# Attention ordered by a list scheduler instead of a table of offsets: a fused attention, mixture and MLP kernel on one core

## The chip, the cores and the metric

The kernel runs on one core of one Trainium2 chip. The metric is the device time of one execution in microseconds (us), from the first to the last instruction on the core with the little that lies around it. Lower is better.

## The reference

The program computes three stages in a row, all in float32:

```
attention: q, k, v of (4 batches, 8 heads, 576 positions, 64), gates f
  scores = q k^T / 8 + cum_i - cum_j        cum = cumsum(log(clip(f)))
  causal mask, softmax over the keys, attn v
x = 2304 tokens x 512                       (heads side by side)
mixture:  P = exp(x w_gate - max); 8 times: rows / sum, columns / sum, * N / E
  out = sum over 8 experts of P[:, e] * (relu(x w1[e]) w2[e])      512 -> 1024 -> 512
MLP:      leaky_relu(out w_in) w_out                               512 -> 2048 -> 512
```

## The kernel before, in words

**Matmul in halves.** TensorE multiplies in a rounded format (`fp32r`), so each float32 operand is kept as a high part and a low part, and a product is three matmuls. Every operand therefore costs a rounding copy (ACT, or a CAST on DVE) and a subtraction (DVE or POOL).

**Attention** runs over 32 heads `n`, one after the other and overlapped. The steps of a head are small functions:

- `qk_load` (DMA), then `k_split` with `k1` and `q1` (CASTs on DVE), `k2` and `q1l` (subtractions on POOL, L392 and L401). A DMA (L396) copies `q1` into another tile.
- `qk` (six score tiles `x`, PE, L444 and L445, into the ring `ps_s` of 4 PSUM tiles), `qk_min` (mask and row minimum, DVE, L456), `qk_exp` (ACT, L469).
- `tr` (four groups `u` of transposes, PE, L495, into the ring `ps_t` of 2 PSUM tiles), `tr_hi` (copy out, ACT, L502), `tr_lo` (low part, DVE, L511, only for heads from 10 on; it is the last reader of the `ps_t` tile).
- `pv` (two groups, PE, L531, in `ps_s`), `pv_copy` (ACT), `pv_add` (DVE, L559, heads from 10 on).

For each pair of heads follow `v_load`, `v_split` (a CAST on DVE, L426, and a subtraction on POOL, L428, pairs from 10 on), `recip` (DVE, L573 to L575), `spread` (POOL, L580), `norm_t` (PE, L589) and `norm_m` (DVE, L595), `x_hi` (ACT), `x_lo` (POOL, L614), `x_store` (DMA), `gate` (PE, L640, L641, in `ps_t`) and `gate_add` (DVE, L649 to L651). Heads below 10 (`EARLY`) multiply in plain float32 in `pv`, and so need no `tr_lo`, `pv_add` and `v_split`.

**Filling products.** The first products of the mixture are cut into 168 pieces of four matmuls, `fill_l1` (L206, 384 columns) and `fill_l2` (L233, 512 columns). Pieces are put between attention's steps so that PE has work while it waits; the ones that are left are scheduled behind attention. Three pieces make a group, whose sum is read by ACT (`high`, or `end`) and DVE (`low` L215, or `end` L239). Their weights are split by ACT (L163) and POOL (L167).

**What sets the order.** The program is written in one order, and each engine works through its own instructions in that order; it waits at each for what it needs. For attention this order comes from tables: each step has an offset in units of a head (`HEAD_E` and `PAIR_E` below head 10, `HEAD_T` and `PAIR_T` from there on), `at(n, t, fn)` puts the step at `n + t`, and all are sorted by that number. Four pieces per head are put at the offsets `FILL_T`, from head 10 on, with their readers (`fill_end`) 0.222 later.

Behind attention (`lg_t`, then the Sinkhorn iterations, then the 56 units of mixture and MLP at L1169) the order is made by a list scheduler, `run_events`: each event has its engine, a duration, its needs and a due time, and the earliest that can start is taken, unless a more urgent one can start soon. That part is not changed.

Of the kernel before, what the change touches and what calls it, by code (L numbers as in the profile page):

```python
# [20 lines left out]
P = 128  # L21
B, H, S, D = 4, 8, 576, 64
# [41 lines left out]

FILL_T = (0.208, 0.376, 0.635, 0.861)
FILL_LAG = 0.222
FILL_FROM = 10


EARLY = 10  # L70
HEAD_E = dict(
    load=-1.126, k1=-0.643, k2=-0.073, q1=-0.639, q1l=-0.339, qk0=-0.040, qk1=0.047,
# [13 lines left out]
FILL_E = (0.05, 0.2, 0.35, 0.5, 0.65, 0.8, 0.95)  # L86


def f(ap):
    return ap.bitcast(F32)  # L90
# [7 lines left out]
def moe_kernel(ctx, tc, qT, kT, v, fg, w_gate, w1, w2, w_in, w_out, out):  # L98
    nc = tc.nc
# [6 lines left out]
    wpa = pool("wpa", 8)  # L106
# [48 lines left out]
    def w_hi(src, pool_):  # L155
        t = pool_.tile([P, 2, FG], F32R, tag="w", name="w")
        hi, lo = t[:, 0, :], t[:, 1, :]
        if len(src.shape) == 3:
            s2 = src.shape[2]
            hv, lv = (t.rearrange("p (k c) -> p k c", c=s2) for t in (hi, lo))  # L160
        else:
            hv, lv = hi, lo
        nc.scalar.activation(hv, src, AF.Copy)  # L163
        return hv, lv

    def w_lo(src, hv, lv):
        nc.gpsimd.tensor_tensor(lv, src, f(hv), ALU.subtract)  # L167
# [50 lines left out]
    fh, fpair, fwait = {}, [], set()  # L218
# [57 lines left out]

    fills = list(fill_steps())

    FIRST = 6 + 2 * (FC + TPB) * 3

    def fill(limit=10 ** 9):
        if fills and n_fills - len(fills) < limit:
            for fn in fills.pop(0)[1]:
                fn()

    n_fills = len(fills)

    def fill_end():
        while pend:
            for fn in pend.pop(0):  # L290
                fn()
        fwait.clear()


    with ExitStack() as actx:
# [79 lines left out]

        ops = {}

        def k_split(n, op):
            rq, rk = raws[n]
# [3 lines left out]
            q1, k1, q2, k2 = ops[n]  # L383
            if op == "k1":
                if n:
                    c_ = ca[n:n + 1] if n == 1 else cd[n]
                    nc.sync.dma_start(out=f(q2[D + 2:D + 4, :]), in_=f(c_))
                    nc.sync.dma_start(out=f(k2[D:D + 2, :]), in_=f(c_))
                nc.vector.tensor_copy(k1, rk)
            elif op == "k2":  # L390
                e = nc.gpsimd if n else nc.vector
                e.tensor_tensor(k2[0:D], rk[0:D], f(k1[0:D]), ALU.subtract)  # L392
            elif op == "q1":
                if n:
                    nc.vector.tensor_copy(q1, rq)
                    nc.sync.dma_start(out=f(q2[0:D]), in_=f(q1[0:D]))  # L396
                else:
                    nc.scalar.activation(q1, rq, AF.Copy)
                    nc.scalar.activation(q2[0:D], rq[0:D], AF.Copy)
            else:  # L400
                (nc.gpsimd if n else nc.vector).tensor_tensor(  # L401
                    q1[D:], rq[D:], f(q1[D:]), ALU.subtract)
# [248 lines left out]
                nc.vector.tensor_tensor(dst, ps[0:2 * E], dst, ALU.add)  # L651


        NH = B * H
        todo = []

        def at(n, t, fn, *args):
            todo.append((n + t, len(todo), fn, args))

        for n in range(NH):  # L660
            T = HEAD_E if n < EARLY else HEAD_T
            if n > 1:
                at(n, T["load"], qk_load, n)
            if n:
                for op in ("k1", "k2", "q1", "q1l"):
                    at(n, T[op], k_split, n, op)
            for x in range(6):
                at(n, T[f"qk{x}"], qk, n, x)
                at(n, T[f"mn{x}"], qk_min, n, x)
                at(n, T[f"ex{x}"], qk_exp, n, x)  # L670
            for u in range(4):
                at(n, T[f"t{u}"], tr, n, u)
                at(n, T[f"hi{u}"], tr_hi, n, u)
                at(n, T[f"lo{u}"], tr_lo, n, u)
            for r in range(2):
                at(n, T[f"pv{r}"], pv, n, r)
                at(n, T[f"cp{r}"], pv_copy, n, r)
                at(n, T[f"ad{r}"], pv_add, n, r)
            if n % 2 == 0:
                T = PAIR_E if n < EARLY else PAIR_T  # L680

                V = PAIR_E if n < EARLY + 4 else T
                if n:
                    at(n, V["vload"], v_load, n)
                for op, fn in (("st", stat), ("rc", recip), ("rb", spread), ("xs", x_hi),
                               ("xl", x_lo), ("xd", x_store)):
                    at(n, T[op], fn, n)
                for op in ("vp", "vl"):
                    at(n, V[op], v_split, n, op)
                for r in range(2):  # L690
                    at(n, T[f"nt{r}"], norm_t, n, r)
                    at(n, T[f"nm{r}"], norm_m, n, r)
                    at(n, T[f"ga{r}"], gate, n, r)
                    at(n, T[f"gb{r}"], gate_add, n, r)
# [4 lines left out]
        at(2, 0.05, gate_prep)  # L699
# [13 lines left out]

        for x, fn in enumerate((lg_t, fill, fill)):
            at(NH, 3.2 + 0.01 * x, fn)
        for _, _, fn, args in sorted(todo, key=lambda x: x[:2]):
            fn(*args)
        fill_end()

# [552 lines left out]
    acc_last, tiles = {}, []  # L1272
    nom = {}

    def fill_main(x, fn):
        fn()
        fwait.clear()
        if pend:
            held[x] = pend.pop()

    def fill_part(x, n):
        held[x][n]()

    held = {}
    S_ = "start"
    for x, (dur, fns) in enumerate(fills):
        for fn in fns:
# [392 lines left out]
```

## Time and profile before

| | |
|---|---|
| three runs | 2028.80, 2029.66, 2029.81 us; median 2029.66 us |
| the profiled execution | 2029.37 us |
| its span (first to last instruction) | 2027.6 us |
| around the span | 1.77 us |
| TensorE's granted clock, mean | 1.000 of full speed |
| matmuls in the trace | 11600 |

"Busy" counts an engine's instructions without gaps. A matmul's end is modelled and overlaps the next one's start, so a gap in PE's work shows shorter than it is; the time from one start to the next is the safer measure. In brackets a row names the idle time ahead of it and what ended it.

### The profile page before, as it was taken

To read this page: it belongs to the slowest core of one execution; us is meant where nothing else is said; L and a number is where in the kernel's file an instruction comes from. 1 tells how busy PE (TensorE), PEld (TensorE's weight loads), DVE (VectorE), ACT (ScalarE), POOL (GpSimd) and SP (SyncE) were. 2 spreads that over 40 slices of the span, in tenths; PEclk is the share of its full clock that TensorE was granted. 3 is DMA by queue.
4 is the path that set the end of the run, shared out by engine and by line. 5 is a ranking of instruction groups with operands and counts; after the bars stand their busy time and mean duration, and the time that the engine had idled before them with its cause. 6 is when DMAs were issued, how large, how long until landed. Compare 5 with 4: busy or idle time off the path is not lost.

```text
span 2027.6 us, 32145 instructions
## 1 busy us (share of the span) xinstructions
PE 1990.3 (98%) x11600; PEld 1941.6 (96%) x11600; DVE 1759.2 (87%) x2423; ACT 983.6 (49%) x1752; POOL 1169.5 (58%) x734
## 2 busy tenths in 40 slices
PE   7999999999999999999999999999999999999999
PEld 6788888999999999999999999999999999999999
DVE  6799985789798999999998989889898989888766
ACT  6887774554444443433343334434333356655443
POOL 4676655646666567666565655656575474455302
PEclk9999999999999999999999999999999999999999
DMA  4654545777887777777767777777677755766563
GB/s 134 176 155 130 152 122 183 271 266 259 271 300 276 242 259 258 244 241 250 245 242 239 274 248 246 248 242 255 239 264 247 249 208 194 263 229 235 182 208 139
DMA packets 145622, 460.54 MB, mean 227 GB/s; under 512 B 15912, under 2 KB 42168, under 8 KB 145464
## 3 DMA queue, kind: packets, MB, share of 16 engines
q1 hardware_dynamic: 145460, 458.48, 66.9%
q8 instruction: 93, 1.52, 0.3%
q14 instruction: 65, 0.53, 0.1%
q10 hardware_dynamic: 4, 0.00, 0.0%
HBM read 402.76 MB, written 51.08 MB: 224 GB/s over the span
## 4 chain that ended last, share of the span: by engine, by line
PE 87%; DVE 9%; issue 2%; ACT 1%; DMA 0%; POOL 0%; SPq 0%; DVEq 0%; ACTq 0%; POOLq 0%
PE x L1169 42%; PE y L1169 32%; PE ps_pv L531 3%; PE ps_m L233 2%; PE ps_t L495 2%; PE ps_m L206 1%; PE ps_s L444 1%; PE ps_s L445 1%; DVE ps_s L456 1%; DVE hl L1240 1%; PE y L233 1%; DVE ptl L511 1%; PE x L206 1%; DVE acc_C L1252 1%; PE y L206 1%
## 5 line engine op out<-in xcount | busy, mean ns | idle before, releaser
L1169 PE MATMUL x<-xw,w 128*128 128x384 f32 x2676 | 500.8, 334 | 2.0 <-DVE xw L923 1.4
L1169 PE MATMUL x<-hh,w 128*128 128x384 f32 x1792 | 490.9, 334 | 2.1 <-DVE w L991 1.7
L1169 PEld LDWEIGHTS x<-xw,w 128*128 128x128 f32 x2676 | 467.0, 188 | 3.7 <-DVE xw L923 2.0
L1169 PE MATMUL y<-xw,w 128*128 128x384 f32 x2004 | 375.0, 334 | 2.6 <-DVE u L1211 1.8
L1169 PE MATMUL y<-hh,w 128*128 128x384 f32 x1344 | 368.0, 334 | 0.0
L1169 PEld LDWEIGHTS y<-xw,w 128*128 128x128 f32 x2004 | 349.5, 188 | 3.6 <-DVE u L1211 2.4
L991 POOL TENSOR_TENSOR w<-wr,w 128x512 fp32r<-128x512 f32 x158 | 251.3, 1595 | 162.6 <-ACT w L163 149.8
L1169 PEld LDWEIGHTS x<-hh,w 128*128 128x128 f32 x1792 | 326.6, 188 | 3.1 <-DVE w L991 2.4
L1169 PE MATMUL x<-hl,w 128*128 128x384 f32 x896 | 299.6, 334 | 1.1 <-DVE hl L1240 0.9
L1169 PEld LDWEIGHTS y<-hh,w 128*128 128x128 f32 x1344 | 245.0, 188 | 0.3 <-issue 0.3
L1169 PE MATMUL y<-hl,w 128*128 128x384 f32 x672 | 224.7, 334 | 0.1
L1252 DVE TENSOR_TENSOR acc_C<-x,acc_C 128x768 f32<-128x768 f32 x177 | 168.4, 952 | 36.6 <-PE x L1169 33.8
L163 ACT ACTIVATE w<-wr 128x512 fp32r<-128x512 f32 x288 | 175.8, 621 | 25.1 <-PE y L1169 17.4
L1252 DVE TENSOR_TENSOR acc_C<-y,acc_C 128x768 f32<-128x768 f32 x148 | 141.0, 953 | 51.9 <-PE y L1169 50.6
L1169 PEld LDWEIGHTS x<-hl,w 128*128 128x128 f32 x896 | 168.2, 188 | 2.0 <-DVE hl L1240 1.5
L1236 ACT ACTIVATE hh<-spare 128x768 fp32r<-128x768 f32 x84 | 71.1, 846 | 147.8 <-PE x L1169 56.9
L1236 ACT ACTIVATE hh<-u 128x768 fp32r<-128x768 f32 x91 | 77.0, 846 | 131.4 <-PE y L1169 82.0
L1240 POOL TENSOR_TENSOR hl<-k,hh 128x768 fp32r<-128x768 f32 x40 | 79.5, 1989 | 97.7 <-ACT hh L1236 97.6
L1236 ACT ACTIVATE hh<-k 128x768 fp32r<-128x768 f32 x112 | 94.7, 846 | 82.3 <-PE x L1169 48.6
L1169 PEld LDWEIGHTS y<-hl,w 128*128 128x128 f32 x672 | 126.1, 188 | 0.7 <-DVE hl L1240 0.7
L1236 ACT ACTIVATE hh<-c 128x768 fp32r<-128x768 f32 x70 | 59.3, 847 | 131.8 <-PE y L1169 82.0
L1205 ACT ACTIVATE u<-x 128x768 f32<-128x768 f32 x91 | 74.1, 814 | 96.1 <-PE x L1169 82.9
(253 smaller groups left out, 3830.4 us busy)
## 6 DMA issues: line engine op xcount, KB each, us to landing
xw<-xo_t SPq DMA_DIRECT2D x208, 768.0 KB
xw<-xo_b SPq DMA_DIRECT2D x154, 768.0 KB
wr<-in_w_dram SPq DMA_DIRECT2D x88, 512.0 KB
pb<-prow SPq DMA_DIRECT2D x44, 384.0 KB
xo_t<-xw SPq DMA_DIRECT2D x16, 768.0 KB
rq<-in_qT_dram SPq DMA_DIRECT2D x64, 144.0 KB
rk<-in_kT_dram SPq DMA_DIRECT2D x64, 144.0 KB
xo_b<-xw SPq DMA_DIRECT2D x12, 768.0 KB
```

The lines of the kernel that those rows point to most:

```text
L163: nc.scalar.activation(hv, src, AF.Copy)
L206: nc.tensor.matmul(ps, w_[:, fs], x_[k][:, xs], start=(x == 0), stop=(x == 11))
L233: nc.tensor.matmul(ps, h_[:, ts], w_, start=(x == 0), stop=(x == 11))
L444: nc.tensor.matmul(o, q1[:, q0:q0 + m], k1[:, k0:k9], start=True, stop=False)
L495: nc.tensor.transpose(ps[:KV[j], c:c + m], prb[n, i][:m, j * P:j * P + KV[j]], ident[:m, :m])
L531: nc.tensor.matmul(ps[:, a - ra:rb - ra], vp, s[:KV[j], o:o + rb - a], start=(x == 0), stop=(x == len(todo) - 1))
L991: ENG[e].tensor_tensor(lo, blk(g, which, WSRC[which][n]), f(hi), ALU.subtract)
L1169: nc.tensor.matmul(o_, w[:, k, w_], m[:, k, :], start=a and k + y == 0, stop=z and k == 1 and y == 2, skip_group_check=True)
L1205: nc.scalar.activation(ctile(u, name, name, bufs), pview(u, p), AF.Copy)
L1236: nc.scalar.activation(hi, tmp[u, LSRC[l]], AF.Copy)
L1240: ENG[e].tensor_tensor(lo, tmp[u, LSRC[l]], f(hi), ALU.subtract)
L1252: nc.vector.tensor_tensor(a, pview(u, l), a, ALU.add)
```

## The change

The tables' offsets no longer set the order. Each step of attention becomes an event `hv(name, how, fn, need, ring, rel, due)`: its engine and duration (`M` PE, `A` ACT, `V` DVE, `P` POOL, `D` DMA; `VP` is DVE using the SBUF port that it shares with POOL), all steps that must be over before it, for PE steps the PSUM ring that it takes a tile of and who releases the tile, and a due time, which is still worked out from the old tables. The pieces and their readers become events of the same kind, with a due time behind all others. `run_heads` then plays the five engines forward: at each turn it takes, over all engines, the event that can start first, where one that is due earlier and can start within a little (`LOOKM` 0.12 us on PE, one instruction elsewhere) goes ahead. Events are then written out in that order.

Two DMAs that were part of `k_split` (`rows`, `q_rows`) become steps of their own. Nothing that is computed changes, and no instruction is added to or taken from PE.

Counted in the order of the two programs on PE: ahead of `lg_t` stand 103 pieces before and 87 now; between the first `qk` of head 11 and the first `qk` of head 31 it is 78 before (48 of `fill_l1`, 30 of `fill_l2`) and 71 now (44 and 27). The other pieces stand behind attention.

Cut to its core:

```diff
-FILL_T = (0.208, 0.376, 0.635, 0.861)
-FILL_LAG = 0.222
-FILL_FROM = 10
+LOOKM, LOOKE = 0.12, 1.0
...
-        def at(n, t, fn, *args):
-            todo.append((n + t, len(todo), fn, args))
...
-                for op in ("k1", "k2", "q1", "q1l"):
-                    at(n, T[op], k_split, n, op)
...
-        for n in range(FILL_FROM, NH + 3):
-            for t in FILL_T if n < NH else FILL_E:
-                at(n, t, fill, FIRST if n < 2 * H + 3 else 10 ** 9)
-                at(n, t + FILL_LAG, fill_end)
...
-        for _, _, fn, args in sorted(todo, key=lambda x: x[:2]):
-            fn(*args)
...
+        BUFS = dict(s=4, t=2, m=2, xt=2)
+        def hv(name, how, fn, *args, need=(), ring=None, rel=(), due=None, t=0.0):
+            hvs[name] = (how, fn, args, [m for m in need if m in hvs], ring, rel, due, t)
...
+                hv(("k1", n), ("VP", 0.39, 0.08), k_split, n, "k1", need=[("load", n)] + old)
+                hv(("k2", n), ("P", 1.41, 0.05), k_split, n, "k2", need=[("k1", n)])
+                hv(("q1", n), ("VP", 0.39, 0.08), k_split, n, "q1", need=[("load", n)] + old)
...
+                hv(("tr", n, u), ("M", M_TR[u], 0.17), tr, n, u,
+                   need=[("ex", n, x) for x in range(6) if XI[x] in TUSE[u]]
+                   + [("pv", n - 2, r) for r in range(2)],
+                   ring="t", rel=[(lo, n, u)], due=place(n, T[f"t{u}"]))
...
+                hv(("lo", n, u), ("V", V_LO[u], 0.07), tr_lo, n, u, need=[("hi", n, u)])
...
+            hv(("rc", n), ("V", 0.5, 0.1), recip, n,
+               need=[("ex", n + y, x) for y in range(2) for x in range(6)])
...
+                    hv(F, ("M", 0.88 if l2_ else 0.71, 0.2), fill_main, x, fn, need=list(dict.fromkeys(need)),
+                       ring="m" if q == 0 else None, rel=[fowner], due=1e6 + x)
...
+        def run_heads():
...
+                        s_ = max(r, free[e])
+                        if how[0] in ("VP", "P"):
+                            s_ = max(s_, port["P" if e == "V" else "V"])
+                        here.append((s_, due[x], x))
...
+                    here.sort(key=lambda k: k[:2])
+                    k = here[0]
+                    for y in here[1:]:
+                        long = hvs[k[2]][0][1]
+                        look = LOOKM if e == "M" else LOOKE * long
+                        if y[1] < k[1] and y[0] < k[0] + look and (e == "M" or y[1] + slip < k[0] + long):
+                            k = y
...
+            for _, x in order:
+                hvs[x][1](*hvs[x][2])
+            return stop
...
+        del fills[:run_heads() + 1]
+        lg_t()
```

Three places show what this does to DVE's queue; lines of the changed kernel have other numbers for the same functions (L453 is `qk_min`, L387 and L393 the CASTs of `k1` and `q1`, L508 `tr_lo`, L646 `gate_add`).

The first place is the start. DVE before, from the end of the part ahead of the loop over heads to the CASTs of head 1 (`k_264`, `q_263`):

```order
L392 TENSOR_TENSOR k_0_227<-rk,k_238 64x576
L456 ISA ps_s,st<-ps_s,mask 96x288
L456 ISA st 96x1
L456 ISA ps_s<-ps_s,mask 96x288
L456 ISA ps_s 96x1
L460 TENSOR_TENSOR st<-st,ps_s 96x1
L389 CAST k_264<-rk 128x576
L395 CAST q_263<-rq 128x576
```

And DVE of the change at the same place, where head 1's tiles are `q_254` and `k_255`:

```order
L390 TENSOR_TENSOR k_0_227<-rk,k_238 64x576
L393 CAST q_254<-rq 128x576
L387 CAST k_255<-rk 128x576
L453 ISA ps_s,st<-ps_s,mask 96x288
L453 ISA st 96x1
```

Head 1's two CASTs moved ahead of head 0's first two `qk_min`.

The second place is head 4, one of the early heads; heads 6 and 8 read alike. DVE before, from the CASTs for head 5 to the first `gate_add` (L649):

```order
L389 CAST k_625<-rk 128x576
L395 CAST q_624<-rq 128x576
L456 ISA ps_s,st<-ps_s,mask 128x128
L456 ISA st 128x1
L456 ISA ps_s,st<-ps_s,mask 128x256
L456 ISA st 128x1
L573 TENSOR_TENSOR st<-st 96x2
L574 TENSOR_SCALAR st<-st 128x10
L575 RECIPROCAL st<-st 128x10
L649 COPY lgT<-ps_g 16x288
```

DVE of the change in head 4, from the same `qk_min` on (`q_706` and `k_707` belong to head 6):

```order
L453 ISA ps_s,st<-ps_s,mask 128x128
L453 ISA st 128x1
L453 ISA ps_s,st<-ps_s,mask 128x256
L453 ISA st 128x1
L646 COPY lgT<-ps_g 16x288
L453 ISA ps_s,st<-ps_s,mask 128x384
L453 ISA st 128x1
L646 COPY lgT<-ps_g 16x288
L453 ISA ps_s,st<-ps_s,mask 96x512
L453 ISA st 96x1
L393 CAST q_706<-rq 128x576
L387 CAST k_707<-rk 128x576
```

CASTs and `recip` no longer stand ahead of `gate_add`; `recip` went to the end of head 3, and the CASTs now serve the head after next. On PE, heads 4 to 9 read the same in both programs.

The third place is head 21, one of the late heads. DVE before, from the end of the first two `qk_min` on (the CAST is for head 22):

```order
L460 TENSOR_TENSOR st<-st,ps_s 96x1
L559 TENSOR_TENSOR xs<-ps_pv,xt 64x320
L456 ISA ps_s,st<-ps_s,mask 128x128
L456 ISA st 128x1
L395 CAST q_2820<-rq 128x576
L511 TENSOR_TENSOR ptl<-ps_t,pth 128x480
L511 TENSOR_TENSOR ptl<-ps_t,pth 128x448
L239 TENSOR_TENSOR acc<-ps_m,acc 128x512
L426 CAST vp<-rv_194 128x5x2x64
L456 ISA ps_s,st<-ps_s,mask 128x256
L456 ISA st 128x1
L511 TENSOR_TENSOR ptl<-ps_t,pth 128x512
```

DVE of the change from the end of head 21's first two `qk_min` on:

```order
L457 TENSOR_TENSOR st<-st,ps_s 96x1
L508 TENSOR_TENSOR ptl<-ps_t,pth 128x480
L508 TENSOR_TENSOR ptl<-ps_t,pth 128x448
L453 ISA ps_s,st<-ps_s,mask 128x256
L453 ISA st 128x1
L453 ISA ps_s,st<-ps_s,mask 128x128
L453 ISA st 128x1
L453 ISA ps_s,st<-ps_s,mask 128x384
L453 ISA st 128x1
L508 TENSOR_TENSOR ptl<-ps_t,pth 128x512
L592 TENSOR_TENSOR xs<-xs,ps_r 128x256
L423 CAST vp<-rv_194 128x5x2x64
```

The CAST of `q1` left its place ahead of `tr_lo`; it stands at the end of head 21 now, right ahead of the next head's first `qk_min`. In heads 18, 20 and 22 the three instructions of `recip` stand between the first two `qk_min`, a few instructions ahead of `tr_lo`.

## Rows read from the trace of the kernel before

**Rows 1.** The page, part 1: busy time of each engine, share of the span, instructions.

```profile
PE 1990.3 (98%) x11600; PEld 1941.6 (96%) x11600; DVE 1759.2 (87%) x2423; ACT 983.6 (49%) x1752; POOL 1169.5 (58%) x734
```

**Rows 2.** Windows: length, then busy PE, PEld, DVE, ACT, POOL (instructions), clock, DMA.

```profile
0.00:8.33 8.33, 0.00 (x0) 0.00 (x0) 5.05 (x10) 4.60 (x6) 4.48 (x16) 1.00 0.58 162
...
23.94:84.17 60.23, 57.91 (x361) 47.44 (x361) 41.56 (x149) 48.10 (x158) 31.43 (x29) 1.00 0.51 144
...
91.86:287.00 195.14, 185.22 (x1223) 165.34 (x1222) 181.55 (x538) 153.39 (x446) 138.22 (x116) 1.00 0.55 148
287.00:318.85 31.85, 31.52 (x188) 28.32 (x188) 17.25 (x45) 17.65 (x41) 13.74 (x11) 1.00 0.33 105
...
345.00:2027.60 1682.60, 1669.54 (x9590) 1660.47 (x9589) 1480.41 (x1582) 732.00 (x1028) 957.43 (x545) 1.00 0.70 243
```

**Rows 3.** Waits of PE from 91.86 to 287: total us, times, longest.

```profile
PE ps_t L495 <- DVE ptl L511: 8.7, 13, 1.3
```

**Rows 4.** Timeline around 190 (POOL, DVE, PE): start, duration, instruction, idle before.

```profile
190.73 1.42 POOL L392 TENSOR_TENSOR k<-rk,k 64x576 fp32r<-64x576 f32 x1
...
190.79 1.68 DVE L395 CAST q<-rq 128x576 fp32r<-128x576 f32 x1
...
192.39 1.18 DVE L511 TENSOR_TENSOR ptl<-ps_t,pth 128x480 fp32r<-128x480 f32 x2
...
193.18 0.63 PE L495 MATMUL ps_t<-ident,p 128*128 128x128 f32 x5 [0.80 <-DVE ptl L511]
```

**Rows 5.** DVE in groups by shape, 91.86 to 287: busy us, mean ns.

```profile
L395 DVE CAST q<-rq 128x576 fp32r<-128x576 f32 x20 | 15.5, 774 | 0.0
...
L389 DVE CAST k<-rk 128x576 fp32r<-128x576 f32 x20 | 12.4, 618 | 0.0
...
L215 DVE SCALAR_TENSOR_TENSOR hl<-ps_m,hh 128x384 fp32r<-128x384 f32 x16 | 8.8, 548 | 0.6 <-ACT hh L214 0.6
...
L573 DVE TENSOR_TENSOR st<-st 96x2 f32<-96x2 f32 x10 | 5.3, 528 | 0.0
```

**Rows 6.** Timeline of DVE, instances of the same instructions elsewhere.

```profile
55.35 0.46 DVE L389 CAST k<-rk 128x576 fp32r<-128x576 f32 x1
55.73 0.45 DVE L395 CAST q<-rq 128x576 fp32r<-128x576 f32 x1
...
56.69 1.14 DVE L573 TENSOR_TENSOR st<-st 96x2 f32<-96x2 f32 x1
...
203.09 0.23 DVE L573 TENSOR_TENSOR st<-st 96x2 f32<-96x2 f32 x1
```

**Rows 7.** Timeline of PE: first qk of heads 6 to 8, and a wait.

```profile
53.70 0.38 PE L444 MATMUL ps_s<-k,q 128*96 128x288 f32 x1
...
58.65 0.38 PE L495 MATMUL ps_t<-ident,p 96*128 96x96 f32 x2 [0.67 <-DVE lgT L651]
...
61.75 0.38 PE L444 MATMUL ps_s<-k,q 128*96 128x288 f32 x1
...
68.94 0.38 PE L444 MATMUL ps_s<-k,q 128*96 128x288 f32 x1
```

**Rows 8.** Timeline of PE: a wait in head 1, first qk of heads 22 and 23.

```profile
15.58 0.56 PE L445 MATMUL ps_s<-k,q 68*96 68x288 f32 x1 [0.68 <-POOL k L392]
...
198.92 0.37 PE L444 MATMUL ps_s<-k,q 128*96 128x288 f32 x1
...
207.65 0.37 PE L444 MATMUL ps_s<-k,q 128*96 128x288 f32 x1
```

**Rows 9.** Timeline of PE behind attention: pieces in a row.

```profile
326.20 2.24 PE L206 MATMUL x<-xp,w 128*128 128x384 f32 x12
328.28 0.85 PE L206 MATMUL y<-xp,w 128*128 128x384 f32 x4
...
339.30 0.39 PE L233 MATMUL y<-w,hl 128*128 128x512 f32 x1
339.53 0.62 PE L233 MATMUL y<-w,hh 128*128 128x512 f32 x2
```

More of the change, by code (lines that the diff above doesn't have):

```diff
@@ L85 @@
 XOPS = ("b11", "b21", "t2", "t3", "t1", "b22", "t4")
-FILL_E = (0.05, 0.2, 0.35, 0.5, 0.65, 0.8, 0.95)
 def f(ap):
@@ L277, in moe_kernel, with fill_main, fill_part @@
     fills = list(fill_steps())
[L279 to L286, printed above, removed]
+    held = {}
+    def fill_main(x, fn):
+        fn()
+        fwait.clear()
+        if pend:
+            held[x] = pend.pop()
+    def fill_part(x, n):
+        held[x][n]()
     def fill_end():
@@ L376, in moe_kernel, with head_ops @@
         ops = {}
-        def k_split(n, op):
-            rq, rk = raws[n]
+        def head_ops(n):
             if n not in ops:
@@ L382, in k_split @@
                           a2.tile([P, S], F32R, tag="k1", name="k1"), q2s[n % 2], k2s[n % 2])
-            q1, k1, q2, k2 = ops[n]
+            return ops[n]
+        def k_split(n, op):
+            rq, rk = raws[n]
+            q1, k1, q2, k2 = head_ops(n)
             if op == "k1":
[L385 to L388, printed above, removed]
                 nc.vector.tensor_copy(k1, rk)
@@ L654, in moe_kernel @@
         NH = B * H
-        todo = []
-        def at(n, t, fn, *args):
-            todo.append((n + t, len(todo), fn, args))
-        for n in range(NH):
[L661 to L664, printed above, removed]
-                for op in ("k1", "k2", "q1", "q1l"):
-                    at(n, T[op], k_split, n, op)
[L667 to L694, printed above, removed]
@@ L695, in moe_kernel, with place @@
-        for n in range(FILL_FROM, NH + 3):
-            for t in FILL_T if n < NH else FILL_E:
-                at(n, t, fill, FIRST if n < 2 * H + 3 else 10 ** 9)
-                at(n, t + FILL_LAG, fill_end)
-        at(2, 0.05, gate_prep)
+        TE, TL = 6.9, 8.6
+        base_of = [TE * min(n, EARLY) + TL * max(n - EARLY, 0) for n in range(NH + 8)]
+        hvs = {}
+        BUFS = dict(s=4, t=2, m=2, xt=2)
+        def place(n, off):
+            x = n + off
+            k = int(x)
+            return base_of[k] + (x - k) * (base_of[k + 1] - base_of[k]) if x > 0 else x * TE
@@ new lines, in hv, with rows, q_rows @@
+        def hv(name, how, fn, *args, need=(), ring=None, rel=(), due=None, t=0.0):
+            assert name not in hvs, name
+            hvs[name] = (how, fn, args, [m for m in need if m in hvs], ring, rel, due, t)
+        def rows(n):
+            c_ = ca[n:n + 1] if n == 1 else cd[n]
+            head_ops(n)
+            nc.sync.dma_start(out=f(ops[n][2][D + 2:D + 4, :]), in_=f(c_))
+            nc.sync.dma_start(out=f(ops[n][3][D:D + 2, :]), in_=f(c_))
+        def q_rows(n):
+            nc.sync.dma_start(out=f(ops[n][2][0:D]), in_=f(ops[n][0][0:D]))
@@ new lines, in run_heads, with offer @@
+        def run_heads():
+            left, succ = {}, {x: [] for x in hvs}
+            for x, v_ in hvs.items():
+                left[x] = len(v_[3])
+                for m in v_[3]:
+                    succ[m].append(x)
+            due = {}
+            for x in reversed(list(hvs)):
+                how, d = hvs[x][0], hvs[x][6]
+                d = 1e6 if d is None else d
+                for y in succ[x]:
+                    d = min(d, due[y] - how[1] - how[2] - 0.1)
+                due[x] = d
+            of_fill = {F for F in fmain.values()} | {m for l in fside.values() for m in l}
+            rest = [x for x in hvs if x not in of_fill]
+            must = set(rest)
+            free = dict(M=0.0, A=0.0, V=0.0, P=0.0, D=0.0)
+            port = dict(V=0.0, P=0.0)
+            over, taken, order, slip = {}, {k: [] for k in BUFS}, [], 0.0
+            cand = {e: {} for e in free}
+            def offer(x):
+                how, _, _, need, _, _, _, t = hvs[x]
+                r = t
+                for m in need:
+                    r = max(r, over[m] + (0.03 if hvs[m][0][0][0] == how[0][0] else 0.1))
+                cand[how[0][0]][x] = r
+            for x in hvs:
+                if not left[x]:
+                    offer(x)
+            stop, owed = None, set()
+            while must or owed:
+                best = None
+                for e in free:
+                    here = []
+                    for x, r in cand[e].items():
+                        if not must and x not in owed:
+                            continue
+                        how, ring = hvs[x][0], hvs[x][4]
+                        if ring and len(taken[ring]) >= BUFS[ring]:
+                            rel = hvs[taken[ring][-BUFS[ring]]][5]
+                            if any(m not in over for m in rel):
+                                continue
+                            r = max([r] + [over[m] + 0.1 for m in rel])
+                        s_ = max(r, free[e])
+                        if how[0] in ("VP", "P"):
+                            s_ = max(s_, port["P" if e == "V" else "V"])
+                        here.append((s_, due[x], x))
+                    if not here:
+                        continue
+                    here.sort(key=lambda k: k[:2])
[5 more added lines that the diff above has]
+                            k = y
+                    if best is None or k[:2] < best[0]:
+                        best = (k[:2], k[2], e)
+                assert best, (len(must), sorted(must, key=lambda x: due[x])[:12], {k: v_[-4:] for k, v_ in taken.items()})
+                (s_, _), x, e = best
+                how, fn, args, _, ring, _, _, _ = hvs[x]
+                if e == "M":
+                    if x in must:
+                        slip = s_ - due[x]
+                del cand[e][x]
+                free[e] = s_ + how[1]
+                over[x] = free[e] + how[2]
+                if how[0] in ("VP", "P"):
+                    port[e] = free[e]
+                if ring:
+                    taken[ring].append(x)
+                must.discard(x)
+                owed.discard(x)
+                order.append((s_, x))
+                if x[0] == "f":
+                    stop = x[1]
+                    owed |= {m for m in fside[stop] if m not in over}
+                if not must and not owed and fills[stop][1][0].args[3] < 2:
+                    owed |= {fmain[stop + 1]} | set(fside[stop + 1])
+                for y in succ[x]:
+                    left[y] -= 1
+                    if not left[y]:
+                        offer(y)
+            for _, x in order:
+                hvs[x][1](*hvs[x][2])
+            return stop
@@ L712, in lg_t @@
                         start=(odd == 0 or j > 0), stop=(odd == 1 or j < half))
-        for x, fn in enumerate((lg_t, fill, fill)):
-            at(NH, 3.2 + 0.01 * x, fn)
-        for _, _, fn, args in sorted(todo, key=lambda x: x[:2]):
-            fn(*args)
-        fill_end()
+        del fills[:run_heads() + 1]
+        lg_t()
     wpc = pool("wpc", WRING - 11)
@@ L1273, in moe_kernel @@
     nom = {}
[L1275 to L1284, printed above, removed]
+    held.clear()
     S_ = "start"
```

127 lines of the change are left out of this document (126 added, 1 removed).

## The prediction

> **What bounds the kernel now.** I read the page first. PE is busy for 98% of the span [rows 1], and the change takes no instruction from it, so the whole gain can only be time in which PE stands. The windows by stage show where that is [rows 2]: in the last 1682.6 us, mixture and MLP, PE stands for 13.1 us, in the first 8.33 us it has nothing to work on, and most of the rest is in attention. The late heads (from the first `qk` of head 11 at 91.86 to that of head 31 at 287.00) take 195.14 us, with PE busy for 185.22, so 9.9 us stand. DVE is at 181.55 of 195.14 there, 93%. The tail of attention (287.00 to 318.85) is dense: 31.52 of 31.85.
>
> The waits say who ends PE's idle time in the late heads: 8.7 of the 9.9 us, in 13 waits, are transposes that wait for `tr_lo` (`ptl`) to free a tile of `ps_t` [rows 3]. The timeline shows why `tr_lo` is late [rows 4]. At 190.73 POOL begins `k2`; at 190.79 DVE comes to the CAST of `q1`, which takes 1.68 us in place of 0.45 in an early head [rows 6], and ends when POOL's 1.42 us and one CAST are over. The two `tr_lo` behind it start at 192.39, and PE waits 0.80 us. The groups show that this is common [rows 5]: the 20 CASTs of `q1` take 774 ns in the mean, those of `k1` 618 where 460 is to be had, and `recip`'s first instruction 528 where one takes 230 [rows 6]. Together DVE loses (0.774 - 0.45) x 20 + (0.618 - 0.46) x 20 + (0.528 - 0.23) x 10 = 6.5 + 3.2 + 3.0 = 12.7 us to waiting for POOL.
>
> **How much PE time can come back in the late heads.** A gap shows too short where ends are modelled, so I go by starts. Pieces in a row: 12 matmuls of `fill_l1` take 328.28 - 326.20 = 2.08 us, so a piece of four is 0.69; one matmul of `fill_l2` takes 339.53 - 339.30 = 0.23, a piece 0.92 [rows 9]. Head 22 runs with no wait: 207.65 - 198.92 = 8.73 us [rows 8] with four pieces of `fill_l1`, so attention's own part of a head is 8.73 - 4 x 0.69 = 5.97. Twenty heads with 48 and 30 pieces are 20 x 5.97 + 48 x 0.69 + 30 x 0.92 = 119.4 + 33.1 + 27.6 = 180.1 us of dense PE work; 195.1 are spent, 15.0 are lost. That is the most the change can win here.
>
> **What the change does, part by part.**
>
> *Start.* The CASTs of head 1 go ahead of head 0's `qk_min`, into time in which DVE waits for the first scores. So POOL's `k2` and `q1l` of head 1 come sooner, and the wait of 0.68 us for `k2` at 15.58 [rows 8] ends. What is next there (PSUM tiles that ACT frees) stays. Gain 0.7 us; the bounds are 0 (the next wait takes it over) and 1.0.
>
> *Early heads.* PE's order in heads 4 to 9 is the same in both, so only the waits can change. Heads 6 and 7 take 61.75 - 53.70 = 8.05 and 68.94 - 61.75 = 7.19 us [rows 7]. Head 6 has the wait of 0.67 us of a transpose for `gate_add`, which stands behind two CASTs and a `recip` of 1.14 us [rows 6]. The change puts both behind it. Heads 4 and 8 are built like head 6. These three should come to the length of an odd one: 3 x 0.86 = 2.6 us. Bounds 0 and 2.6.
>
> *Late heads.* The CAST leaves its place ahead of `tr_lo`, and the scheduler counts the port that DVE and POOL share. What a head then takes, p, is bounded from both sides. PE: attention's 5.97 plus the change's 71 pieces, (20 x 5.97 + 44 x 0.69 + 27 x 0.92) / 20 = 8.73 us. DVE: its 181.55 us less the 12.7 lost to POOL is 168.9; the seven pieces fewer take with them a third of a `low` each (0.548 / 3 [rows 5]), 1.3 us; 167.6 / 20 = 8.38. But `recip` has no port in the scheduler's list (`V`, not `VP`) and waited in the old order; if each of the ten meets half of a POOL instruction like that of 1.42 us [rows 4], that is 0.36 per head. DVE also stands for 13.6 us now, 0.68 per head, waiting for PE and ACT; I keep half of it, 0.34, since a list made from durations shortens such waits but can't end them. So p = 8.38 + 0.36 + 0.34 = 9.1 us, 0.66 under today's 9.76. The bounds are 8.73 (PE dense) and 9.76 (nothing won).
>
> *The pieces.* Seven fewer in the late heads cost 4 x 0.69 + 3 x 0.92 = 5.5 us behind them; PE does the same work elsewhere. So a shorter head is not all gain: 20 x 0.66 = 13.2 us less 5.5 is 7.7. The other nine of the sixteen that leave attention are neutral while the tail stays dense. There the tail's own chain (last `pv`, `norm_m`, `x_lo`, `gate`) has fewer pieces for cover; I take 0, and 2 us if one POOL instruction of that chain lies open.
>
> *DMAs.* The `rows` and `q_rows` transfers are steps of their own, issued up to a head sooner than now on SP's queue. They are covered by that lead; without it PE's next `qk` would wait. All of PE's gaps in the late heads that are not for `ptl` come to 9.9 - 8.7 = 1.2 us [rows 2, 3], which is the most that such transfers can cost now, and I price them at nothing.
>
> *Behind attention.* Mixture and MLP keep their order but for the 16 added pieces; 13.1 us of gaps there may move by 2 either way. I take 0.
>
> The sum on the profiled execution, 2029.4 (span 2027.6 and 1.8 around it): with 0.7 and 2.6 off, T = 2029.4 - 3.3 - (195.1 - 20p) + 5.5 = 1836.5 + 20p. For p = 9.1 that is 2018.5 us. The runs' median is 0.3 above the profiled one: **2018.8 us**.
>
> **A rule that speaks against it.** In the trace `recip`'s first instruction takes 1.14 us in one place and 0.23 in another [rows 6]. The Trainium skill's page "SBUF — State Buffer", section "Who interferes with whom", says that a DVE instruction with two SBUF inputs contends with a GpSimd instruction that reads SBUF, and that the loser blocks for the other's whole length. By that rule, the trace agrees; it would put `recip` under the port, where the scheduler's list has it free. At the old order's mean of 528 ns [rows 5] `recip` costs (0.528 - 0.23) / 2 = 0.15 per head, p would be 8.38 + 0.15 + 0.34 = 8.87 and T 2013.9; with a block of a whole POOL instruction per pair it is rival 2, 2025.3. I stand between the two.
>
> **The rivals.**
>
> 1. *The waits all go.* The new order has no CAST ahead of `tr_lo`, and 8.7 of the 9.9 us hang on that. p = 8.73: 2011.1, with the median 2011.4. Against it: DVE would have to run at (8.38 + 0.15) / 8.73 = 98% even with `recip` as it is now.
>
> 2. *The port takes it back through `recip`.* In the even heads `recip` now stands between the first two `qk_min`, just ahead of `tr_lo`, where the CAST stood in spirit. If each waits a whole POOL instruction, 1.42 us, and PE stands as long, p = 8.73 + 1.42 / 2 = 9.44: 1836.5 + 188.8 = 2025.3, 2025.6 with the median. For it: the 1.14 us [rows 6]. Against it: POOL is busy for 138.22 of 195.14 us [rows 2], so some waits are short. The rule above is this rival's.
>
> 3. *Slower: POOL's queue falls behind the plan.* POOL and the CASTs together hold the port for 138.2 / 20 + 0.46 + 0.45 = 7.8 us of each head's 9.1, 86%. In the new order `k2`, `q1l`, `x_lo` and the weights' low parts stand in POOL's queue as planned; where one is late, all behind it are, and PE stands at a `pv` or a `qk` that waits for POOL. One POOL instruction of 1.42 us late in each head in place of today's wait gives p = 8.73 + 1.42 = 10.15, 2039.5. It decides from p = 9.66 (2029.7), and is measurably slower from p = 9.86. For it: a fixed order has no slack. Against it: PE's gaps for all but `ptl` come to only 1.2 us in the late heads now [rows 2, 3].
>
> 4. *It does nothing*: another instruction ahead of `tr_lo` is as late as the CAST was. p = 9.5 to 9.6, 2026.8 to 2028.8.
>
> **How the numbers follow.** My forecast (p from 8.9 to 9.3, 2014.8 to 2022.8) has a chance of 0.5; rival 1 (p below 8.9) 0.2; rivals 2 and 4 (9.3 to 9.66) 0.2 together; rival 3 0.1. A difference of 0.2%, 4.1 us, is about what a measurement here can tell from no change. Faster than 2025.6 is the forecast, rival 1 and over half of rivals 2 and 4: 0.81. Within 4.1 us: the rest of these and a little of rival 3, 0.12. Slower than 2033.7: 0.07. The range for 8 in 10 leaves the ends of rivals 1 and 3 outside: 2010 to 2027.
>
> **What would show it.** If I am right, the wait of PE for `ptl` in the late heads falls from 8.7 to under 4 us, the CASTs of `q1` and `k1` come near 0.46 us each, the time from head 11's to head 31's first `qk` is about 182 us, PE's waits for `lgT` in heads 4 to 8 are gone, and `lg_t` comes some 20 us before its 318.85 [rows 2], since 16 pieces more follow it. I am wrong if CASTs or `recip` in front of `tr_lo` still take over 0.7 us, if PE shows waits for POOL, or if gaps appear between attention and the mixture, where the cover is thinner.

## The result, and the profile after

The changed kernel takes 2041.82 us (median of 4 runs, 2040.38 to 2043.63) against 2029.74 for the kernel before: a ratio of 1.0061, 95% interval 1.0043 to 1.0078. It is slower by 12 us, where 2018.8 was forecast. The profiled execution took 2041.69 us, with a span of 2039.9.

The page, part 1, of the changed kernel, in the form of [rows 1]:

```profile
PE 1996.0 (98%) x11600; PEld 1947.4 (95%) x11600; DVE 1767.0 (87%) x2426; ACT 981.2 (48%) x1752; POOL 1163.1 (57%) x731
```

PE has the same 11600 matmuls. It stands for 2039.9 - 1996.0 = 43.9 us in place of 37.3, which is half of the loss; its busy time has grown by 5.7 us, and that too wants an explanation. The windows, cut as in [rows 2] (early heads, late heads, tail of attention, behind it):

```profile
23.94:96.39 72.45, 66.62 (x407) 54.65 (x405) 53.59 (x171) 54.74 (x178) 41.24 (x38) 0.98 0.52 142
96.39:293.97 197.58, 183.59 (x1194) 164.23 (x1193) 181.93 (x531) 149.27 (x443) 128.49 (x112) 0.97 0.50 141
293.97:318.30 24.33, 24.10 (x149) 21.22 (x149) 17.09 (x46) 12.84 (x32) 10.09 (x8) 1.00 0.27 84
345.00:2039.90 1694.90, 1682.64 (x9658) 1672.65 (x9656) 1479.85 (x1587) 737.94 (x1038) 953.02 (x543) 1.00 0.70 241
```

Head 11 begins at 96.39 (before 91.86), so the start and the early heads lost 4.5 us. The late heads take 197.6 us, p = 9.88, where 182 was forecast, and with seven pieces fewer in them than before. `lg_t` comes at 318.3, half a microsecond sooner than before, though 16 pieces now stand behind it; what is behind it takes 12.9 us more (2041.7 - 318.3 less 2029.4 - 318.85), as 9 pieces of 0.69 and 7 of 0.92 should (12.7). The granted clock, 1.00 everywhere before, is 0.97 in the late heads.

The next view shows DVE in groups by shape in the late heads (busy us, mean ns), to set against [rows 5]:

```profile
L570 DVE TENSOR_TENSOR st<-st 96x2 f32<-96x2 f32 x10 | 10.6, 1061 | 0.0
L387 DVE CAST k<-rk 128x576 fp32r<-128x576 f32 x19 | 9.1, 480 | 0.0
L571 DVE TENSOR_SCALAR st<-st 128x10 f32<-128x10 f32 x10 | 8.8, 878 | 1.0
L393 DVE CAST q<-rq 128x576 fp32r<-128x576 f32 x19 | 8.6, 451 | 0.2
L572 DVE RECIPROCAL st<-st 128x10 f32<-128x10 f32 x10 | 2.2, 216 | 0.3
```

The CASTs are where they were forecast, at 451 and 480 ns. But `recip`'s sum went from 528 to 1061 ns, and its second instruction, which adds EPS, takes 878. In the kernel before, over all 16 pairs, that second one (L574 there) never waited:

```profile
L573 DVE TENSOR_TENSOR st<-st 96x2 f32<-96x2 f32 x16 | 11.3, 705 | 0.0
L574 DVE TENSOR_SCALAR st<-st 128x10 f32<-128x10 f32 x16 | 2.8, 174 | 0.6
```

The timeline of the change in a late head, around 204, shows how it comes about:

```profile
202.23 1.42 POOL L398 TENSOR_TENSOR q<-rq,q 64x576 fp32r<-64x576 f32 x1 [0.55 <-ACT xth L607]
...
202.44 1.22 DVE L570 TENSOR_TENSOR st<-st 96x2 f32<-96x2 f32 x1
...
203.72 1.42 POOL L611 TENSOR_TENSOR xtl<-xs,xth 128x576 fp32r<-128x576 f32 x1
203.76 1.41 DVE L571 TENSOR_SCALAR st<-st 128x10 f32<-128x10 f32 x1
...
205.34 0.44 DVE L453 CUSTOM_DVE_ANT_0 ps_s<-ps_s,mask 96x288 f32<-96x288 f32 x1
...
205.89 1.18 DVE L508 TENSOR_TENSOR ptl<-ps_t,pth 128x480 fp32r<-128x480 f32 x2
206.06 0.50 ACT L466 ACTIVATE p<-ps_s,st 96x288 f32<-96x288 f32 x1 [2.20 <-DVE st L457]
...
206.68 0.89 PE L492 MATMUL ps_t<-ident,p 128*128 128x128 f32 x7 [1.74 <-DVE ptl L508]
```

The sum meets POOL's `q1l` and waits until it ends. In the gap before DVE's next instruction POOL begins `x_lo`, 0.04 us ahead of the EPS addition, which waits for the whole of that too. Instructions of 0.15 and 0.17 us hold DVE from 202.44 to 205.17, the second `qk_min` and both `tr_lo` stand behind them, and PE waits 1.74 us.

The two traces also show what lets POOL in. In the old order the EPS addition starts 0.03 to 0.04 us after the end of the sum, in all 16 pairs, and that is just soon enough: in 7 of them POOL begins its own next instruction 0.02 to 0.03 us later. This is the pair of the 1.14 us in [rows 6]:

```profile
57.87 0.17 DVE L574 TENSOR_SCALAR st<-st 128x10 f32<-128x10 f32 x1
57.90 1.42 POOL L392 TENSOR_TENSOR k<-rk,k 64x576 fp32r<-64x576 f32 x1
```

In the change the EPS addition follows the last exponentials so closely that the program makes it wait for ACT as well, whose row sums it reads. DVE gets an instruction for this wait in 15 of the 16 pairs, the addition then starts 0.11 us or more after the sum, and POOL is in before it in 13 of these. In the 16th pair, without that wait, it gets through:

```profile
L571 DVEq EVENT_SEMAPHORE  x15: 21/21/21, 23.7 to 302.1; - x15
...
264.41 1.04 DVE L570 TENSOR_TENSOR st<-st 96x2 f32<-96x2 f32 x1
...
265.49 0.17 DVE L571 TENSOR_SCALAR st<-st 128x10 f32<-128x10 f32 x1
265.51 1.42 POOL L611 TENSOR_TENSOR xtl<-xs,xth 128x576 fp32r<-128x576 f32 x1
```

No run changes this wait alone, so its share is read from the traces and not measured.

Head 4, an early head, has the same with POOL's two subtractions behind the CASTs (`q1l`, then `k2`):

```profile
38.51 1.42 POOL L398 TENSOR_TENSOR q<-rq,q 64x576 fp32r<-64x576 f32 x1 [0.54 <-DVE q L393]
38.58 1.37 DVE L570 TENSOR_TENSOR st<-st 96x2 f32<-96x2 f32 x1
40.01 1.40 POOL L390 TENSOR_TENSOR k<-rk,k 64x576 fp32r<-64x576 f32 x1
40.05 1.39 DVE L571 TENSOR_SCALAR st<-st 128x10 f32<-128x10 f32 x1
...
43.40 0.92 PE L528 MATMUL ps_pv<-pt,rv 128*128 128x256 f32 x4 [2.00 <-ACT p L466]
...
45.99 3.57 PE L528 MATMUL ps_pv<-pt,rv 128*128 128x320 f32 x10
```

Here ACT's exponentials wait for the `qk_min` behind `recip`, and `pv` for them. The last row shows the second effect. The same ten matmuls took 2.49 us in the kernel before, at 44.10:

```profile
44.10 2.49 PE L531 MATMUL ps_pv<-pt,rv 128*128 128x320 f32 x10
```

and the windows of the change around it give the granted clock, which had been 1.00:

```profile
41.00:45.00 4.00, 2.00 (x14) 1.70 (x13) 2.74 (x13) 2.25 (x9) 1.25 (x3) 0.97 0.52 148
45.00:50.00 5.00, 5.00 (x19) 3.49 (x17) 2.16 (x7) 2.60 (x10) 2.30 (x2) 0.69 0.14 31
```

PE was busy for half of 41 to 45, and from then on matmuls run for a stretch at the lower level, 1.2 GHz, in place of 2.4. There are five such stretches between 40 and 325 in this execution, and none in that of before. That is where busy time grew, by 1.1 us in these ten matmuls alone.

These are PE's waits in the late heads, the group that answers to [rows 3], with the next after it:

```profile
PE ps_t L492 <- DVE ptl L508: 10.8, 8, 2.2
...
PE ps_s L441 <- DVE xs L556: 2.1, 2, 1.7
```

Fewer waits for `ptl` than before, 8 for 13, but of up to 2.2 us, and 10.8 us in all where 8.7 was to fall below 4.

### The profile page after: what moved, and what is told of

Read it like the earlier page. It is cut to its first block, busy times and chain, and to the rows that moved or that the text cites. A ratio compares the mean times of both kernels' runs of the same rounds, so it can differ in the third digit from the quotient of the medians.

```text
span 2039.9 us, 32131 instructions
## 1 busy us (share of the span) xinstructions
PE 1996.0 (98%) x11600; PEld 1947.4 (95%) x11600; DVE 1767.0 (87%) x2426; ACT 981.2 (48%) x1752; POOL 1163.1 (57%) x731
## 4 chain that ended last, share of the span: by engine, by line
PE 85%; DVE 8%; ACT 2%; DMA 2%; issue 2%; POOL 0%; SPq 0%; DVEq 0%; ACTq 0%; POOLq 0%
PE x L1382 43%; PE y L1382 32%; PE ps_pv L528 1%; PE ps_m L230 1%; PE ps_t L492 1%; PE y L230 1%; PE y L203 1%; DVE ps_s L453 1%; PE ps_s L441 1%; PE x L203 1%; PE x L230 1%; PE ps_s L442 1%; ACT p L466 1%; DVE hl L1453 1%; PE ps_m L203 1%
## 5 line engine op out<-in xcount | busy, mean ns | idle before, releaser
L1204 POOL TENSOR_TENSOR w<-wr,w 128x512 fp32r<-128x512 f32 x161 | 255.7, 1592 | 165.4 <-ACT w L160 152.7
L1453 POOL TENSOR_TENSOR hl<-k,hh 128x768 fp32r<-128x768 f32 x35 | 69.0, 1973 | 83.3 <-ACT hh L1449 83.3
```

The lines of the kernel that those rows point to most:

```text
L1204: ENG[e].tensor_tensor(lo, blk(g, which, WSRC[which][n]), f(hi), ALU.subtract)
L1453: ENG[e].tensor_tensor(lo, tmp[u, LSRC[l]], f(hi), ALU.subtract)
```

## The experiments

The experiments set two theories against each other. **Theory A**: the loss is `recip`'s two waits for POOL. **Theory B**: they cover other waits of the new order, and the loss would stay without them. To tell them apart, `recip` is made so that neither instruction is there: its sum becomes a `tensor_reduce`, and the addition of EPS (1e-9) is left out.

```
-nc.vector.tensor_tensor(st[:m, 0, 4], st[:m, 2, 2], st[:m, 2, 3], ALU.add)
-nc.vector.tensor_scalar(rs, rs, EPS, None, ALU.add)
+nc.vector.tensor_reduce(
+    st[:m, 0, 4], st[:m, 2, 2:4].rearrange("p a b -> p b a"), axis=AX.X, op=ALU.add)
```

**The change with this `recip`.**

> The changed kernel in the same order, with recip in a form that reads one SBUF operand: the sum of the two halves by a tensor_reduce, and the addition of 1e-9 left out (the sums are at least 1, so float32 drops it). Theory A, recip waits for POOL twice per pair and PE behind it: the 23.1 us that L570 and L571 spend over their least on DVE go, PE's gaps over 1 us in heads 2 to 30 go, the granted clock is 1.000 again, and the time is 2012 to 2024 us. Theory B, the new order is slow in itself (fewer pieces for cover, queues in the wrong order): DVE's waits only move, PE's gaps of 1 to 2 us stay, and the time stays at 2034 us or over.

It takes 2022.11 us (2021.20 to 2023.21), a ratio to the kernel before of 0.9961 (0.9947 to 0.9976): theory A. The sum now takes 145 ns in the mean of 16 pairs (138 to 149), with no wait for POOL, so this form is called port-free below:

```profile
L570 DVE TENSOR_REDUCE st<-st 96x2 f32<-96x4 f32 x16 | 2.3, 145 | 0.0
```

The windows of the early and late heads:

```profile
23.94:89.28 65.34, 64.67 (x410) 53.99 (x408) 47.02 (x165) 54.44 (x179) 41.90 (x38) 1.00 0.57 157
89.28:274.30 185.02, 180.83 (x1193) 163.07 (x1193) 165.15 (x520) 148.31 (x443) 128.71 (x111) 0.98 0.53 150
```

Head 11 begins 7.1 us sooner than in the change, and the late heads are 12.6 us shorter: 19.7 us, all of the difference between the two programs (2041.8 - 2022.1). DVE's busy time in the late heads falls by 16.8 us. Two things that were expected did not come: the granted clock is 0.98 in the late heads and not 1.00, and one wait of PE over 1 us is left (1.56 us at 103.35, for ACT's `p`).

**The old order with this `recip`.**

> The kernel before in its own order with the same recip. Theory A: there L573 spends 9.0 us over its least, in 5 early and some late pairs, and stands ahead of gate_add and two places ahead of tr_lo, so the three waits of PE for gate_add shrink from 0.67 and some late ones go: 2021 to 2027 us. It gains less than the changed kernel does from the same edit. Theory B: recip is no matter in either kernel, 2028 to 2031 us.

It takes 2024.21 us (2023.50 to 2026.14), 0.9972 (0.9962 to 0.9982). In the old order these waits cost 6 us, in the new one 20. And with neither in the way the new order is worth 2.1 us (2022.1 against 2024.2), not the 11 of the forecast. Heads 4, 6 and 8 of the old order now take 7.2 to 7.3 us each.

**The change with the EPS addition left out, its sum still a `tensor_tensor`.**

```
-nc.vector.tensor_scalar(rs, rs, EPS, None, ALU.add)
```

> The changed kernel in the same order with the addition of 1e-9 left out and the tensor_tensor kept, so that recip has one instruction that can meet POOL in place of two. Theory A, two waits in a row make it: DVE loses about 11 us in place of 23, no gap of PE comes near 2 us, the clock stays at 1.000, and the time is 2018 to 2030 us. A rival within A, that one wait ahead of tr_lo is as bad as two: 2034 to 2042 us. Theory B: 2038 to 2042 us.

It takes 2024.19 us (2023.23 to 2026.78), 0.9973 (0.9963 to 0.9983). The sum still takes 870 ns in the mean of all 16 pairs, as in the change. The window of the late heads:

```profile
90.22:278.10 187.88, 180.84 (x1194) 161.60 (x1193) 172.79 (x520) 148.94 (x443) 128.21 (x111) 0.99 0.52 148
```

So one wait per pair costs 2.1 us, with the late heads at 187.9 for 185.0, and the second one 17.6.

**The change with the sum as `tensor_reduce`, the EPS addition kept.** Does the EPS addition wait by itself, or only behind another?

> The change with only recip's first instruction made a tensor_reduce; the tensor_scalar that adds EPS stays. Theory A (the tensor_scalar waits for POOL by itself, whatever stands ahead of it): it takes about 0.9 us in the mean in place of 0.17, as a single port wait, and the time is near the 2024.2 of after_one, where the other of the two was kept. Theory C (it waits only because the tensor_tensor ahead let a POOL instruction in between; alone it is free): 172 ns each, and 2022, as after_reduce. If two port instructions in a row are not what cost 17 us, the time stays near 2036 to 2040.

It takes 2028.79 us (2024.74 to 2031.51, 11 runs), 0.9988 (0.9979 to 0.9997). The EPS addition waits by itself:

```profile
L572 DVE TENSOR_SCALAR st<-st 128x10 f32<-128x10 f32 x16 | 13.6, 849 | 3.1 <-ACT p L466 1.9
```

Either instruction alone gives away part of the 20 us (2.1 or 6.7); two in a row cost more than both. The time is not near the 2024.2 that was expected. Part of the 6.7 us goes with the granted clock: the run with a mean of 1.000 took 2024.74 us, the four with 0.997 took 2029.35 to 2031.51.

**The change with `recip` listed under the port.** The scheduler's entry for `recip` says `VP` for `V`, and 0.62 for 0.5.

```
-hv(("rc", n), ("V", 0.5, 0.1), recip, n,
+hv(("rc", n), ("VP", 0.62, 0.1), recip, n,
```

> The changed kernel with one word and one number of the scheduler's list changed: recip as VP with 0.62 us, so that it is placed when POOL is idle. All instructions as in the change. Theory A: the waits of L570 and L571 fall from 23.1 to under 6 us, the clock is 1.000, and the time is 2013 to 2026 us. Theory B: 2034 us or over; a new order, but with the same weakness.

It takes 2024.83 us (2021.52 to 2028.63, 10 runs), 0.9975 (0.9965 to 0.9984). The two instructions take 8.7 us in 16 pairs, for 28.2 in the change. One entry of the scheduler's list, with every instruction still there, turns the loss of 12 us into a gain of 5. What is left are single waits of PE of 1.3 to 1.6 us.

**The old order with `recip` moved.** This puts the suspected cost into the old kernel, without anything else of the change: the late heads' `recip` goes between the first two `qk_min`, where the change has it.

```
-    st=-0.607, vload=-1.477, vp=-0.550, vl=1.120, rc=2.607, rb=2.898, ...
+    st=-0.607, vload=-1.477, vp=-0.550, vl=1.120, rc=2.230, rb=2.898, ...
```

> The old order with recip (all three instructions) of the late heads moved from 2.607 to 2.230, that is to between the first two qk_min, where the change has it. Theory A (the place, a few instructions ahead of tr_lo and with POOL at its CAST parts, is what makes recip dear): L573 and L574 take 0.7 us or more in the mean each and PE stands longer for ptl: 2032 to 2038 us. Rival (recip's place does not matter; the loss is in the rest of the new order): 2028 to 2031, with L574 at 173 ns as before.

It takes 2040.20 us (2038.44 to 2040.76), 1.0047 (1.0034 to 1.0060), above the range that was expected: one number in the old kernel's table costs 10 us, nearly what the whole change lost. The groups, over all pairs:

```profile
L573 DVE TENSOR_TENSOR st<-st 96x2 f32<-96x2 f32 x16 | 13.8, 863 | 0.0
...
L574 DVE TENSOR_SCALAR st<-st 128x10 f32<-128x10 f32 x16 | 10.2, 635 | 1.3
```

The timeline around 248 shows the EPS addition caught although the sum ahead of it ran free:

```profile
247.39 0.15 DVE L573 TENSOR_TENSOR st<-st 96x2 f32<-96x2 f32 x1
247.52 1.28 POOL L167 TENSOR_TENSOR w<-wr,w 128x512 fp32r<-128x512 f32 x1 [0.24 <-ACT w L163]
247.65 1.18 DVE L574 TENSOR_SCALAR st<-st 128x10 f32<-128x10 f32 x1
...
249.73 0.50 ACT L469 ACTIVATE p<-ps_s,st 96x288 f32<-96x288 f32 x1 [1.61 <-DVE st L460]
```

The late heads take 205.2 us there, with the clock at 1.00, so waits alone can cost this much:

```profile
93.17:298.36 205.19, 188.23 (x1223) 165.06 (x1222) 187.79 (x538) 151.61 (x446) 137.52 (x116) 1.00 0.52 140
```

PE's waits for `ptl` hardly grow there (9.4 us for 8.7); those for `xs`, the `pv_add` behind, go from 0.6 to 7.1 us.

**The old order with port-free `recip`, and the CAST of `q1` moved beside that of `k1`** (`q1=-0.924` for `-0.648` in `HEAD_T`). The forecast held that CAST for the cause of PE's waits in the old order.

> The old order with the same port-free recip (2024.2 alone) and one offset changed: the CAST of q1 in late heads goes next to that of k1 (-0.924 for -0.648), so that it stands ahead of POOL's k2 and not behind. Theory A (PE's 6.5 us of waits for ptl in that program hang on the CAST that is caught by k2 right ahead of tr_lo): CASTs of q1 near 0.5 us, waits for ptl under 3 us, 2018 to 2021 us, better than both programs. Rival (the place only shifts the stall: with the CAST gone another DVE instruction ahead of tr_lo is late): waits for ptl stay over 5 us, 2023 to 2026.

It takes 2024.47 us (2024.22 to 2027.12), 0.9974 (0.9964 to 0.9985), against 2024.21 without the move. Waits for `ptl` in the late heads fall from 6.2 to 1.4 us, as theory A had it, but the time doesn't follow, as the rival had it. PE's waits there:

```profile
PE ps_s L444 <- DVE xs L559: 2.0, 3, 1.2
...
PE ps_t L495 <- DVE ptl L511: 1.4, 6, 0.2
PE ps_s L444 <- ACT p L469: 1.2, 1, 1.2
```

The CAST is caught in its new place too, by `x_lo`, and at 1023 ns in the mean of the late heads (750 without the move) it is dearer than before:

```profile
233.66 0.44 DVE L389 CAST k<-rk 128x576 fp32r<-128x576 f32 x1
233.75 1.63 POOL L614 TENSOR_TENSOR xtl<-xs,xth 128x576 fp32r<-128x576 f32 x1 [5.70 <-ACT xth L610]
234.03 1.67 DVE L395 CAST q<-rq 128x576 fp32r<-128x576 f32 x1
```

What is late next is the `qk_min` and `pv_add` behind it: PE's waits for `xs` go from 0.8 to 2.0 us, and one of 1.2 us for ACT's `p` and one of 0.7 for `lgT` appear. The late heads take 191.5 us, for 191.7 without the move. What a CAST that meets POOL nowhere would win, this run can't say.

**The change with port-free `recip` and a length near its true one in the list** (0.33 for 0.5; the reduce and the reciprocal take 142 and 217 ns).

> The change with recip that needs no port (its sum as a tensor_reduce, no EPS), as in the experiment after_reduce, and the scheduler's list told its new length (0.33 for 0.5). Theory A (the port waits were the loss, the list is sound): a true length helps a little, 2019 to 2022 us, head 11 to head 31 in 182 to 185 us. Rival (what is left of the loss is where the list happens to put things, and any new length deals anew): anything from 2020 to 2026, with gaps of 0.5 to 1.5 us for ACT's p at other heads than before, and no better than the 2022.1 of after_reduce.

It takes 2018.78 us (2017.75 to 2019.69), 0.9943 (0.9930 to 0.9955): faster than both kernels. Its late heads take 177.9 us, under the 182 to 185 that were expected, but with 40 pieces of `fill_l1` in them for 44, so the length dealt a new order too. That the time is the 2018.8 of the forecast is chance: this is another program. Two lengths between the two ask if that is the truth of the number or the luck of a new order:

> As after_fit (2018.8 us), but the list is told 0.42 for recip, neither its true length nor the 0.5 of after_reduce (2022.1). Theory A (a true length is what helped): between the two, 2019 to 2022, gaps where they had them. Rival (each length deals the instructions anew, and the 3.3 us between the two are a lucky deal): outside that stretch, by up to 3 us either way.

> As after_fit, with 0.45. Theory A: 2020 to 2022, nearer to after_reduce. Rival (a deal): outside that stretch, or better than after_042 though less true.

They take 2021.42 us (2019.52 to 2022.53, ratio 0.9957, 0.9945 to 0.9970) and 2022.21 (2019.38 to 2024.07, 0.9962, 0.9948 to 0.9975). The row 0.33, 0.42, 0.45, 0.5 gives 2018.8, 2021.4, 2022.2, 2022.1. That fits theory A, but the last three differ by less than these runs can tell, and that 0.33 was merely dealt a good order is not ruled out.

## Why the prediction was wrong, by its steps

**Late heads** is the step that failed: p = 9.88 for 9.1, 15.6 of the 23 us by which the forecast missed. Its CAST half held (451 and 480 ns for 0.46). Two terms of its sum, 8.38 + 0.36 + 0.34 per head, were too small. The first is `recip`'s, half a POOL instruction per pair: its two instructions each wait for a POOL instruction, 1061 and 878 ns in the mean where 146 and 172 are the least, which is 16.2 us in ten pairs, 0.81 per head for 0.36. The second is the time in which DVE waits for PE and ACT. The list was to halve it to 0.34; it is 197.58 - 181.93 = 15.65 us, 0.78 per head. The rest of DVE's work, 8.29, is near the 8.38.

The experiment says what the first of these is worth in time: without `recip`'s waits the late heads are 12.6 us shorter, 5.4 more than the 7.2 of the term. The other 10.2 us of the 15.6 are in the rest of the sum. Without `recip` the sum would have said 8.73, dense PE, 174.6 us; the change with port-free `recip` takes 185.0, p = 9.25. Of these 10.4 us PE stands for 4.2, and the clock of 0.98 takes up to 3.7 (2% of 185); where the other 2.5 or so are isn't shown (modelled ends can hide waits). For the change itself the same account gives 23.0 us over dense: 14.0 standing, up to 5.9 at the lower clock (3% of 197.6), and about 3 not shown. The granted clock was in no term: the forecast took every matmul at the durations of a kernel that had it at 1.00.

**"8.7 of the 9.9 us hang on that"** is a reading that the move of one CAST in the old order speaks against: the row of waits names who ended PE's idle time, not what would come back. Most of the waits for `ptl` went, other waits came, and the late heads stayed as long.

**A rule that speaks against it** and **rival 2** had the mechanism, but not its size. Rival 2 priced one whole POOL instruction per pair at p = 9.44 and 2025.3 us. With one of the two instructions left the runs give 187.9 / 20 = 9.39 and 2024.2, but that these meet is luck: rival 2 sets 0.71 for the wait on a dense 8.73, and the runs set 0.14 on the 9.25 that are there without any wait. What it missed is the second instruction. I took L574 for free since the trace had it at 0.17 us each time; it was free because in the old place POOL did not begin an instruction between the two, often by a mere 0.02 to 0.03 us. The Trainium skill's page "SBUF — State Buffer", section "Who interferes with whom", names that instruction too: `tensor_scalar`, copies and casts can enter a mode that takes both ports, while `tensor_reduce` never contends on this chip. The runs agree with both (172 up to 1408 ns for the one, 136 to 150 for the other); I had used only its sentence on two inputs.

**Early heads** failed the same way: 4.4 us lost from head 4 on, where 2.6 were to be won. PE's order is the same, and its waits for `lgT` in heads 4 to 8 are gone; but `recip`, moved to the end of the odd head, met both `q1l` and `k2` there, and head 4 took 10.9 us. In heads 6, 8 and 10 (8.4 to 8.5 us) the sum runs free, and the EPS addition alone waits, for 0.81 to 0.89 us. With port-free `recip` head 11 begins 2.6 us sooner than before, of the 3.3 that start and early heads were to win. That heads 4, 6 and 8 of the old order fall to 7.2 us with port-free `recip` alone (7.3 for head 8) shows that their 0.86 us were `recip`'s, not the CASTs'.

**Start** was right in its wait (POOL's `k2` is no longer waited for at 15.6), but head 4 begins at 38.58 for 38.46: the first pair's `recip` took the 0.7 us. **Pieces** and **DMAs** were right: 16 pieces cost what they were priced at, and no wait of PE between 24 and 330 is for a DMA. **Behind attention**: PE stands 0.55 us for DVE's copy of the gate's logits where the cover got thin, and one stretch at the lower clock follows at 321; in all, 12.9 us for 12.7 of pieces, so the 0 that was taken held. **Rival 3** named a time near the one that came, 2039.5, by another road: the trace of the change has no wait of PE for POOL at all between 24 and 330.

Open: what makes ACT's `p` late in the change with port-free `recip` (2.6 of the 4.2 us that PE stands there, in three waits; 1.2 more are for `xs`), and how much of the lower clock's cost is the gaps' and how much chance, since executions of one program differ by 2 to 7 us.

## What to carry to other kernels

Before a DVE instruction is moved, look at what POOL does at the new place, and price every instruction of the group that can want the port at up to a whole POOL instruction, however short it is. Look also at what each of them waits for: in the old order POOL got in between no two that ran 0.03 to 0.04 us apart, and in the change it got in 13 times where a wait for ACT made that 0.11 or more (at 0.03 us too it did once, at 194 in the change with `recip` listed under the port). "It never waited in this trace" is a fact on its place, not on the instruction; a scheduler needs it listed as one that takes the port, or written so that it takes none. And a wait that is taken away gives back only what the next instruction in the queue doesn't lose: compare periods from start to start, not sums of waits.

## What was not expected of the hardware

An addition on 128x10 elements, 172 ns alone, took up to 1408 ns, and it lost the port to the next POOL instruction right after the sum ahead of it had waited for the one before: 2.7 us from 202.44 on, for 0.3 us of work. A second surprise is TensorE's clock in a program that keeps it 98% busy: after waits of 2.00 us (43.40) and 1.74 us (206.68) the granted clock went to the lower level, and ten matmuls took 3.57 us in place of 2.49. It did not after every such wait: behind one of 2.16 us at 107.83 and one of 2.05 us at 247.80 it stayed at 1.00. Nor does it take one: in the change with the EPS addition left out the clock is 0.51 from 215.6 to 219 behind a wait of 1.0 us, and in the change with port-free `recip` 0.50 from 213.0 to 216.4 behind three of 0.5, 0.3 and 0.3. Waits as long in sum, in short pieces (the old order with `recip` moved, 17 us of standing in the late heads, the longest 1.2 us), left the clock at 1.00 in the profiled execution. What makes it fall is therefore not settled here.
